# Attention and two feed-forward layers: weight sums moved between engines, attention paced denser, PSUM banks shared earlier

## The chip, the cores and the metric

The kernel runs on one core of a Trainium2 chip. The metric is the device time of one execution in microseconds. Three runs of the kernel before gave 716.2, 716.98 and 717.67 us; the median is 716.98. One more execution was taken with the profiler.

## The reference

Three stages, in float32, each feeding the next:

```python
# attention: B, H, S, D = 2, 8, 768, 64; six sign bits per row choose a bucket
mask = q_bucket[:, :, :, None] == k_bucket[:, :, None, :]
scores = np.where(mask, scale * q @ k.T, -1e9)
attn = exp(scores - max) / (sum + 1e-9)
x = (attn @ v) as 1536 tokens x 512
# layer 1: 512 -> 2048 -> 512
h = x @ w_in;  g = where(h > 0, h, exp(min(h, 0)) - 1);  x = g @ w_out
# layer 2: 512 -> 2048 -> 512
h = x @ w_in2; g = s * max(h, 0)**2 + b;                 out = g @ w_out2
```

The inputs arrive as float64 words. The kernel reads them as pairs of 32-bit integers and rebuilds float32 from them on the chip.

## The kernel before, in words

**Precision.** Every matmul of the layers works on operands split into two float16 parts, high and low. Three products (high x high, high x low, low x high) stand for one. ScalarE mostly writes the high part (a copy to float16), and VectorE or GpSimd writes the low part (the value minus the high part).

**Attention** goes in 96 units of 128 queries of one head. `u_s` (L352) computes the scores s into PSUM, `u_soft` (L362) takes them out on VectorE with the maximum (L368) and applies the exponential on ScalarE (L370), `u_split` (L374) writes ph as high part on ScalarE (L389) and low part on GpSimd (L392) and sends a transposing DMA from SP's queue, and `u_av` (L397) multiplies with v into xacc (L412). `u_norm` (L425) finishes 128 tokens. Units 48 to 95 are batch 1.

**Layer 1** (`moe1`, L627) goes in six blocks of 256 tokens, each `up(i)` and then `down(i)`, both in 16 slots of 12 matmuls on TensorE (L533). A pair of slots of `up` fills one PSUM tile h; `act1` (L536) turns it into g: e on ScalarE (L541 and, in blocks 0, 1, 4 and 5, its scaling L543), g on VectorE (L550), the high part gh on ScalarE (L553), the low part gl on GpSimd (L556). A `down` fills two PSUM tiles x2p in 8 slots each, and ScalarE writes each to x (L676). The PSUM tiles h and x2p come from a ring of pools (`Ring`, L117, kind "m"); it has three banks from the time that layer 1's weights are decoded.

**Weaving.** After each slot, `model_kernel` (L1049 on) adds the slot's cost to a credit, and runs half units of attention for half of `sc` each. `sc` is 1.2 for the first 16 slots, then `STEP_COST` 2.5:

```python
cost = 12 * (n / 2400 + .003)
credit += cost
sc = STEP_COST if ks >= SC_N else SC0
while live["att"] and credit >= sc / 2 and may_step():
    credit -= sc / 2
    att_step()
```

The order on each engine is made when the program is built, by a list scheduler that goes by readiness and by a priority, which is the place in the program. So the weave sets priorities, and what is ready can go ahead.

**Layer 2's weights.** Once attention is exhausted, its pools are closed, four PSUM pools `ps_y` are opened (before, only layer 2 used them), and a stream `ws2` of 32 chunks begins (`w_stream`, L170). A step of it loads one chunk (a DMA of SP, three buffers), decodes the chunk loaded two steps earlier with three VectorE instructions (L194, L195, L197; a "triple" below), and takes the one decoded in the step before. A step is taken in two of seven slots until `F0` = 18 steps are made. All of a step's instructions have their priority put back by `D2` = 200 places.

`wo_chunks` (L711) and `wi_chunks` (L738) say what taking means. Layer 2 is computed with seven block products in place of eight, so its weights are needed as blocks and as four sums of blocks. Two chunks make a pair. ScalarE scales each chunk (L716, L743). Then four 128x256 sums go into a tile tt, which has one buffer (L725 to L728 for w_out2, L751 to L754 for w_in2), all on GpSimd. Then high and low parts are written in three pieces of 256, 512 and 1024 columns for w_out2 (L733 and L734; the first two low parts on VectorE, the last, from tt, on GpSimd) and of 512, 256 and 1024 for w_in2 (L758 and L759, all low parts on GpSimd). Eight pairs of w_out2 and eight of w_in2 are made. The converted w_in2 tile has two buffers.

**Layer 2's x operands.** `x_piece` (L591) makes the sums of x blocks (L607) and low parts (L604) on VectorE and the high parts on ScalarE (L601). They are written over layer 1's weights `wi`, so each waits until up(5) has read what it overwrites. The last of them wait for the end of layer 1.

**Layer 2.** `up2` (L765) runs eight blocks j of 14 products (L809), six banks in use; the first product of each side also presets a bank (L814). After each product it takes steps of the weight stream up to a goal between `fed_at[j]` and `fed_at[j+1]`. `finish` (L782) and `product` (L801) empty the banks on ScalarE (L788, L816, L819) and VectorE (L796, L821, L825). The banks are the list `ps_m + ps_y` in this order: a of both sides, c of both, b of both. `down2` (L870) then makes the output (L948).

Of the kernel before, what the change touches and what calls it, by code (L numbers as in the profile page):

```python
# [12 lines left out]
ALU = mybir.AluOpType  # L13
# [33 lines left out]
GUEST = [(0, "k"), (0, "q"), (2, "k"), (2, "q"), (0, "v"), (1, "v")]  # L47
NS = 2
NX = 1
F0 = 18  # L50
Y2 = 4
D2 = 200
DA = 4
# [4 lines left out]
WEV = lambda k: k % 3  # L58
W2EV = lambda k: k % 7 in (0, 3)
STEP_COST = 2.5  # L60
SC0 = 1.2
SC_N = 16
PRE = 4
# [4 lines left out]
def model_kernel(tc, q, k, v, proj, w_in, w_out, w_in2, w_out2, s2, b2, sel, pop, eye, out):  # L68
    nc = tc.nc
# [23 lines left out]
    with ExitStack() as base:  # L93
# [21 lines left out]
        ps_m = []  # L115
# [25 lines left out]
        ring = Ring()  # L141
# [329 lines left out]
        nxt = {"s": 0, "av": 0, "soft": [], "split": [], "lag": LAG0}  # L471
# [239 lines left out]
        def wo_chunks(dram, wq, lp):  # L711
            w = dram.bitcast(I32)
            kept = {}

            def take(f, a):
                nc.scalar.activation(out=a, in_=a, func=ACTF.Copy, scale=SW)  # L716
                kept[f] = a
                if f < KF // 2:
                    return
                f -= KF // 2  # L720
                a, c = kept.pop(f), kept.pop(f + KF // 2)
                b11, b12, b21, b22 = a[:, :256], a[:, 256:], c[:, :256], c[:, 256:]
                t = lp.tile([128, 4, 256], F32, tag="tt", name="tt")
                t1, n2, t3, n4 = (t[:, x, :] for x in range(4))
                nc.gpsimd.tensor_tensor(out=t1, in0=b12, in1=b11, op=ALU.subtract)  # L725
                nc.gpsimd.tensor_tensor(out=n2, in0=t1, in1=b22, op=ALU.subtract)
                nc.gpsimd.tensor_tensor(out=t3, in0=b22, in1=b12, op=ALU.subtract)
                nc.gpsimd.tensor_tensor(out=n4, in0=b21, in1=n2, op=ALU.add)  # L728
                hi, lo = wq
                c = c.rearrange("p (x n) -> p x n", x=2)  # L730
                for eng, o, src in ((nc.vector, slice(0, 1), a[:, None, :256]), (nc.vector, slice(1, 3), c),
                                    (nc.gpsimd, slice(3, 7), t)):
                    nc.scalar.activation(out=hi[:, o, f, :], in_=src, func=ACTF.Copy)  # L733
                    eng.tensor_tensor(out=lo[:, o, f, :], in0=src, in1=hi[:, o, f, :], op=ALU.subtract)  # L734
            order = [f for x in range(KF // 2) for f in (x, x + KF // 2)]
            return [(lambda a, f=f: take(f, a), w[128 * f:128 * f + 128, :]) for f in order]

        def wi_chunks(dram, wt, lp, wjp):  # L738
            w = dram.bitcast(I32)
            kept = {}  # L740

            def take(f, a):
                nc.scalar.activation(out=a, in_=a, func=ACTF.Copy, scale=SW)  # L743
                kept[f] = a
                if f % 2 == 0:
                    return
                a, c = kept.pop(f - 1), kept.pop(f)
                a11, a12, a21, a22 = a[:, :256], a[:, 256:], c[:, :256], c[:, 256:]
                t = wjp.tile([128, 4, 256], F32, tag="tt", name="tt")
                s1, m2, s3, s4 = (t[:, x, :] for x in range(4))  # L750
                nc.gpsimd.tensor_tensor(out=s1, in0=a21, in1=a22, op=ALU.add)  # L751
                nc.gpsimd.tensor_tensor(out=m2, in0=a11, in1=s1, op=ALU.subtract)
                nc.gpsimd.tensor_tensor(out=s3, in0=a11, in1=a21, op=ALU.subtract)
                nc.gpsimd.tensor_tensor(out=s4, in0=a12, in1=m2, op=ALU.add)  # L754
                o = wt[f // 2] = lp.tile([128, 2, 7, 256], F16, tag="wi2", name="wi2", bufs=2)
                a = a.rearrange("p (x n) -> p x n", x=2)
                for x, src in ((slice(0, 2), a), (slice(2, 3), a22[:, None, :]), (slice(3, 7), t)):
                    nc.scalar.activation(out=o[:, 0, x, :], in_=src, func=ACTF.Copy)  # L758
                    nc.gpsimd.tensor_tensor(out=o[:, 1, x, :], in0=src, in1=o[:, 0, x, :], op=ALU.subtract)  # L759
            return [(lambda a, f=f: take(f, a), w[:, 256 * f:256 * f + 256].rearrange("(k p) n -> p k n", p=128))  # L760
                    for f in range(KF)]
# [3 lines left out]
        def up2(wt, home, g, g3, banks, stream, fed, fed_all, ahead):  # L765
# [67 lines left out]
            def quads(j):  # L833
                Qs = [dict(j=j, p=p, banks={}, pools={}) for p in range(2)]
                for x in "acb":
                    for Q in Qs:
                        Q["pools"][x] = free.pop(0)
                        Q["banks"][x] = Q["pools"][x].tile([128, 512], F32, tag="m", name=x + "2")[:, :NT]
                return Qs
# [2 lines left out]
            std = [(x, n) for n in (1, 5, 6, 2, 7, 3, 4) for x in range(2)]  # L842
            begin = [(0, 1), (1, 1), (0, 5), (1, 5), (0, 6), (0, 2), (1, 2), (1, 6), (0, 7), (0, 3), (1, 7), (0, 4), (1, 3), (1, 4)]
            end = [(0, 1), (0, 5), (1, 1), (0, 6), (0, 2), (1, 5), (0, 7), (1, 6), (0, 3), (0, 4), (1, 7), (1, 2), (1, 3), (1, 4)]
            fed_at = [F0, 22, 24, 28, 30, 32, 34, 36, 36]
            step, over = 0, False
            for j in range(N8):
                Qs = quads(j)
                for e, (x, n) in enumerate(begin if j == 0 else end if j == N8 - 1 else std):
                    product(Qs[x], n)  # L850
                    for o in range(4):
                        run(o)
                    tick()
                    goal = fed_at[j] + (fed_at[j + 1] - fed_at[j]) * (e + 1) // 14
                    if j == 6:
                        goal = min(36, 34 + e)
                    while not over and fed[0] < goal:
                        if next(stream, 0) == 0:
                            over = True
                            fed_all()  # L860
                        fed[0] += 1
                    if j == N8 - 1 and e == 9:
                        ahead(3)
# [126 lines left out]
        if True:  # L990
# [59 lines left out]
            for ks, cost in enumerate(moe1(wi, wo, gp, next_gp, tmp, tmpg, att_step, home)):  # L1050
                if WEV(ks):
                    w1_step()
                credit += cost
                sc = STEP_COST if ks >= SC_N else SC0
                while live["att"] and credit >= sc / 2 and may_step():
                    credit -= sc / 2
                    att_step()
                if not live["att"] and ws2 is None:
                    exst.close()
                    ast.close()  # L1060
                    ps_y = [pool(pst, f"ps_y{i}", 1, space=PSUM) for i in range(Y2)]
                    wqp = right(wqst, "wq", 1)
                    wq = [wqp.tile([128, 7, KF // 2, DM // 2], F16, name=f"wq{x}") for x in "hl"]
                    lp = right(late, "late", 1)
# [9 lines left out]
                    sb["s"], sb["b"], sb["2b"] = (sbs[:, x:x + 1] for x in range(3))  # L1074
                    co = wo_chunks(w_out2, wq, wjp)
                    ci = wi_chunks(w_in2, wi2, lp, wjp)
                    ch = co[:10] + ci[:4] + co[10:14] + ci[4:8] + co[14:] + ci[8:]
                    ws2 = w_stream(ch, wraw,
                                   lambda: (wjp.tile([128, 512], F32, tag="wa", name="wa", bufs=3),
                                            ps_x.tile([128, 512], F32, tag="x", name="wx")), delay=D2)  # L1080
                elif ws2 is not None and W2EV(ks) and fed2[0] < F0:
                    next(ws2)
# [81 lines left out]
```

## Time and profile before

| | |
|---|---|
| median of three runs | 716.98 us (716.2 to 717.67) |
| profiled execution, its own time | 716.12 us |
| its span, first to last instruction | 714.3 us |
| mean granted TensorE clock | 0.983 |
| busy: TensorE matmuls | 647.5 us (91%) |
| busy: VectorE, ScalarE, GpSimd | 528.0, 474.0, 376.2 us (74%, 66%, 53%) |

The span is what the engines' instructions cover; 1.8 us of the execution's time lie around it. Busy times overlap between engines. A matmul's end is modelled and reaches into the next one, so a TensorE that is busy all the time is not one at its peak, but one that waits for nothing. The granted clock is a share of full speed: 1.00 is 2.4 GHz, and a mean below it says that for a part of the stretch the clock stood at 1.2 GHz. In the rows, "a <- b" is the tile written and the tiles read; at the end of a row, "<-" names what ended the idle time before it.

### The profile page before, as it was taken

To read this page: it belongs to the slowest core of one execution; us is meant where nothing else is said; L and a number is where in the kernel's file an instruction comes from. 1 tells how busy PE (TensorE), PEld (TensorE's weight loads), DVE (VectorE), ACT (ScalarE), POOL (GpSimd) and SP (SyncE) were. 2 spreads that over 40 slices of the span, in tenths; PEclk is the share of its full clock that TensorE was granted. 3 is DMA by queue.
4 is the path that set the end of the run, shared out by engine and by line. 5 is a ranking of instruction groups with operands and counts; after the bars stand their busy time and mean duration, and the time that the engine had idled before them with its cause. 6 is when DMAs were issued, how large, how long until landed. Compare 5 with 4: busy or idle time off the path is not lost.

```text
span 714.3 us, 15720 instructions
## 1 busy us (share of the span) xinstructions
PE 647.5 (91%) x6290; PEld 514.0 (72%) x6290; DVE 528.0 (74%) x876; ACT 474.0 (66%) x810; POOL 376.2 (53%) x323
## 2 busy tenths in 40 slices
PE   2789779888889899999999998877999999999998
PEld 0368657767667688888888886664566667888887
DVE  5688899888888568645742599999777667999820
ACT  2897679863798888656756667756677677556410
POOL 1257778873445479756854488886577741000000
PEclk9999979999999999999999999999999999999999
DMA  9974699999899698676759554223234002301011
GB/s 233 264 218 137 164 210 248 206 204 254 153 205 215 105 166 162 130 123 112 127 111 124 144 175 144 60 67 110 88 119 150 23 34 82 129 30 46 30 42 34
DMA packets 209625, 96.05 MB, mean 134 GB/s; under 512 B 172176, under 2 KB 205712, under 8 KB 209552
## 3 DMA queue, kind: packets, MB, share of 16 engines
q1 hardware_dynamic: 208960, 94.92, 59.3%
q8 instruction: 49, 0.80, 0.4%
q14 instruction: 24, 0.20, 0.1%
q10 hardware_dynamic: 592, 0.14, 0.1%
HBM read 46.27 MB, written 6.29 MB: 74 GB/s over the span
## 4 chain that ended last, share of the span: by engine, by line
PE 46%; DVE 8%; ACT 6%; issue 3%; POOL 2%; DMA 1%; SPq 0%; DVEq 0%; ACTq 0%; POOLq 0%
PE y L948 15%; PE a L809 8%; PE x2p L533 6%; PE h L533 5%; PE c L809 4%; PE s L358 3%; PE xacc L412 3%; PE b L809 2%; DVE x L607 1%; DVE e L548 1%; DVE wil L604 1%; ACT p L370 1%; ACT ph L389 1%; DVE wx L195 1%; DVE wa L197 1%
## 5 line engine op out<-in xcount | busy, mean ns | idle before, releaser
L392 POOL TENSOR_TENSOR ph<-p,ph 128x768 f16<-128x768 f32 x80 | 132.8, 1665 | 69.0 <-ACT ph L389 50.3
L533 PE MATMUL h<-x,wih 128*128 128x256 f16 x768 | 133.8, 278 | 4.7 <-DVE g L550 4.6
L368 DVE TENSOR_SCALAR_CACHE_REDUCE p<-s 128x768 f32<-128x768 f32 x96 | 91.2, 952 | 57.9 <-PE s L358 54.0
L370 ACT ACTIVATE p<-p,mx 128x768 f32<-128x768 f32 x96 | 89.2, 929 | 49.9 <-DVE mx L369 43.5
L533 PE MATMUL x2p<-gh,woh 128*128 128x256 f16 x384 | 103.8, 273 | 3.7 <-DVE g L550 2.7
L533 PE MATMUL h<-x,wil 128*128 128x256 f16 x384 | 106.6, 278 | 0.0
L533 PE MATMUL x2p<-gl,woh 128*128 128x256 f16 x384 | 104.3, 273 | 1.7 <-POOL gl L556 1.7
L533 PE MATMUL x2p<-gh,wol 128*128 128x256 f16 x384 | 104.4, 273 | 1.2 <-DVE wol L204 1.2
L809 PEld LDWEIGHTS <-wi 128*128 128x128 f16 x672 | 66.3, 99 | 49.0 <-issue 7.0
L533 PEld LDWEIGHTS <-wih 128*128 128x128 f16 x768 | 75.5, 100 | 20.4 <-DVE g L550 6.7
L533 PEld LDWEIGHTS <-woh 128*128 128x128 f16 x768 | 74.6, 98 | 16.4 <-issue 3.9
L358 PE MATMUL s<-k,q 128*128 128x512 f16 (+1 forms) x384 | 80.8, 336 | 4.6 <-DVE p L368 4.3
L412 PE MATMUL xacc<-vv,pt 128*128 128x64 f16 x1440 | 57.9, 195 | 18.9 <-DMA pt<-ph 18.8
L556 POOL TENSOR_TENSOR gl<-g,gh 128x512 f16<-128x512 f32 x48 | 59.2, 1233 | 28.5 <-ACT gh L553 27.9
L412 PEld LDWEIGHTS <-pt 128*128 128x128 f16 x1440 | 53.7, 99 | 26.5 <-DMA pt<-ph 23.3
L389 ACT ACTIVATE ph<-p 128x768 f16<-128x768 f32 x80 | 66.4, 836 | 5.7 <-DMA pt<-ph 4.8
L358 PEld LDWEIGHTS <-q 128*128 128x128 f16 x384 | 34.4, 100 | 23.1 <-issue 9.2
L194 DVE TENSOR_SCALAR wx<-wraw 128x512 int32<-128x512 int32 x64 | 44.5, 695 | 5.7 <-DMA wraw<-in_moe_w_out 5.0
L197 DVE SCALAR_TENSOR_TENSOR wa<-wraw,wx 128x512 int32<-128x512 int32 x64 | 43.7, 682 | 5.1 <-POOL wi L759 2.3
L809 PE MATMUL a<-wih,wi 128*128 128x384 f16 x160 | 46.3, 329 | 1.2 <-ACT x L676 1.2
L195 DVE SCALAR_TENSOR_TENSOR wx<-wraw,wx 128x512 int32<-128x512 int32 x64 | 44.2, 691 | 0.9
L533 PEld LDWEIGHTS <-wol 128*128 128x128 f16 x384 | 37.6, 98 | 8.0 <-issue 2.0
(186 smaller groups left out, 1536.0 us busy)
## 6 DMA issues: line engine op xcount, KB each, us to landing
wraw<-in_moe_w_in SPq DMA_DIRECT2D x32, 512.0 KB, 3.8
wraw<-in_moe_w_out SPq DMA_DIRECT2D x32, 512.0 KB, 4.2
g<-x SPq DMA_DIRECT2D x16, 192.0 KB, 1.9
x<-g SPq DMA_DIRECT2D x4, 768.0 KB, 5.2
out<-y SPq DMA_DIRECT2D x10, 256.0 KB, 2.0
raw<-in_k SPq DMA_DIRECT2D x6, 384.0 KB, 4.5
raw<-in_q SPq DMA_DIRECT2D x6, 384.0 KB, 4.9
v<-in_v SPq DMA_DIRECT2D x4, 384.0 KB, 4.7
```

The source lines that it names most:

```text
L195: nc.vector.scalar_tensor_tensor(out=x, in0=low, scalar=29, in1=x, op0=ALU.logical_shift_right, op1=ALU.bitwise_or)
L197: nc.vector.scalar_tensor_tensor(out=a, in0=top, scalar=-0x40000000, in1=x, op0=ALU.bitwise_and, op1=ALU.bitwise_or)
L358: nc.tensor.matmul(p[:, a0:a1], w[b, hp][:, j, c, :], kf[:, a0:a1], start=(x == 0), stop=(x == 1))
L368: nc.vector.tensor_scalar(f, sps.pop(u), CLAMP, None, op0=ALU.min, op1=ALU.min, accum_out=mx)
L370: nc.scalar.activation(out=f, in_=f, func=ACTF.Exp, scale=-sm / (SQ * SQ), bias=mx, accum_out=sums[b, c][:, h:h + 1])
L389: nc.scalar.activation(out=t[:, 0, :], in_=f, func=ACTF.Copy)
L392: nc.gpsimd.tensor_tensor(out=t[:, 1, :], in0=f, in1=t[:, 0, :], op=ALU.subtract)
L412: nc.tensor.matmul(acc, o[:, C * x + cc, :], vv[:, j, cc, y, :], start=(z == 0 and cc == 0), stop=(z == 2 and cc == C - 1))
L533: nc.tensor.matmul(p, ws[a](kk), xs[b](kk), start=(kk == 0 and z == 0), stop=(kk == n_kk - 1 and z == 2))
L556: nc.gpsimd.tensor_tensor(out=gl, in0=t["g"], in1=gh, op=ALU.subtract)
L809: nc.tensor.matmul(d, w[:, wz, WI[n], kk * 128:kk * 128 + 128], home[p, xn, xz][:, kk, :], start=first and k == 0, stop=k == 3 * K1 - 1, s ...
L948: nc.tensor.matmul(p, a[:, xa, kk, :], wq[y][:, WQ[n], kk, :], start=first and k == 0, stop=k == 3 * K2 - 1, skip_group_check=True)
```

## The change

- The four sums of each w_out2 pair go from GpSimd to VectorE; the first two low parts of the pair go from VectorE to GpSimd.
- The four sums of the first two w_in2 pairs (f = 1 and 3) go from GpSimd to VectorE.
- From unit 60 on a unit of attention costs 2.0 credits in place of 2.5.
- When attention is exhausted, the ring of layer 1's PSUM tiles gets `ps_m + ps_y`, seven banks in place of three, and its count starts anew.
- Layer 2's chunks come in another order after the first 14: two of w_out2 and two of w_in2 in turn, in place of four and four.
- 17 steps of the stream in place of 18 ahead of `up2`; within `up2` the goal after block 0 is 20 in place of 22, and goals are reached earlier within a block (rounded up instead of down, nearly).

```diff
-F0 = 18
+F0 = 17
...
+SC2, U2 = 2.0, 60
...
-                nc.gpsimd.tensor_tensor(out=t1, in0=b12, in1=b11, op=ALU.subtract)
-                nc.gpsimd.tensor_tensor(out=n2, in0=t1, in1=b22, op=ALU.subtract)
-                nc.gpsimd.tensor_tensor(out=t3, in0=b22, in1=b12, op=ALU.subtract)
-                nc.gpsimd.tensor_tensor(out=n4, in0=b21, in1=n2, op=ALU.add)
+                nc.vector.tensor_tensor(out=t1, in0=b12, in1=b11, op=ALU.subtract)
+                nc.vector.tensor_tensor(out=n2, in0=t1, in1=b22, op=ALU.subtract)
+                nc.vector.tensor_tensor(out=t3, in0=b22, in1=b12, op=ALU.subtract)
+                nc.vector.tensor_tensor(out=n4, in0=b21, in1=n2, op=ALU.add)
...
-                for eng, o, src in ((nc.vector, slice(0, 1), a[:, None, :256]), (nc.vector, slice(1, 3), c),
+                for eng, o, src in ((nc.gpsimd, slice(0, 1), a[:, None, :256]), (nc.gpsimd, slice(1, 3), c),
                                     (nc.gpsimd, slice(3, 7), t)):
...
-                nc.gpsimd.tensor_tensor(out=s1, in0=a21, in1=a22, op=ALU.add)
-                nc.gpsimd.tensor_tensor(out=m2, in0=a11, in1=s1, op=ALU.subtract)
-                nc.gpsimd.tensor_tensor(out=s3, in0=a11, in1=a21, op=ALU.subtract)
-                nc.gpsimd.tensor_tensor(out=s4, in0=a12, in1=m2, op=ALU.add)
+                eng = nc.vector if f < 4 else nc.gpsimd
+                eng.tensor_tensor(out=s1, in0=a21, in1=a22, op=ALU.add)
+                eng.tensor_tensor(out=m2, in0=a11, in1=s1, op=ALU.subtract)
+                eng.tensor_tensor(out=s3, in0=a11, in1=a21, op=ALU.subtract)
+                eng.tensor_tensor(out=s4, in0=a12, in1=m2, op=ALU.add)
...
-            fed_at = [F0, 22, 24, 28, 30, 32, 34, 36, 36]
+            fed_at = [F0, 20, 24, 28, 30, 32, 34, 36, 36]
...
-                    goal = fed_at[j] + (fed_at[j + 1] - fed_at[j]) * (e + 1) // 14
+                    goal = fed_at[j] + ((fed_at[j + 1] - fed_at[j]) * (e + 1) + 11) // 14
...
-                sc = STEP_COST if ks >= SC_N else SC0
+                sc = SC0 if ks < SC_N else STEP_COST if nxt["s"] < U2 else SC2
...
+                    ring.use(m=ps_m + ps_y)
...
-                    ch = co[:10] + ci[:4] + co[10:14] + ci[4:8] + co[14:] + ci[8:]
+                    ch = co[:10] + ci[:4] + co[10:12] + ci[4:6] + co[12:14] + ci[6:8] + co[14:16] + ci[8:10] + ci[10:12] + ci[12:14] + ci[14:16]
```

## Rows read from the trace of the kernel before

**Rows 1.** Windows: stretch, length, busy us (instructions) per engine, clock, DMA share, GB/s.
```profile
255.00:300.00 45.00, 43.51 (x563) 36.30 (x561) 33.86 (x68) 35.16 (x63) 38.27 (x26) 1.00 0.90 159
...
400.00:429.50 29.50, 29.50 (x271) 26.31 (x269) 25.82 (x43) 19.70 (x34) 21.41 (x20) 1.00 0.62 193
429.50:486.00 56.50, 46.01 (x394) 38.94 (x392) 54.62 (x66) 37.15 (x62) 48.40 (x39) 0.97 0.29 88
486.00:500.00 14.00, 9.82 (x48) 5.06 (x46) 13.90 (x23) 8.91 (x19) 8.28 (x9) 0.88 0.37 112
500.00:520.00 20.00, 20.00 (x125) 11.96 (x123) 14.02 (x26) 12.38 (x28) 9.72 (x10) 1.00 0.31 99
520.00:560.00 40.00, 40.00 (x248) 24.09 (x247) 30.93 (x55) 28.85 (x58) 30.95 (x32) 1.00 0.35 109
```

The engines of a window stand in the order PE, PEld, DVE, ACT, POOL.

**Rows 2.** Waits of PE, 425 to 500 us: total us, times, longest.
```profile
PE h L533 <- DVE g L550: 4.6, 3, 2.9
PE x2p L533 <- DVE g L550: 2.7, 1, 2.7
PE b L809 <- DVE wih L604: 2.0, 1, 2.0
PE b L814 <- ACT wih L601: 1.9, 1, 1.9
PE a L809 <- ACT x L676: 1.2, 1, 1.2
PE x2p L533 <- POOL gl L556: 0.9, 1, 0.9
PE c L809 <- DVE wih L604: 0.6, 1, 0.6
```

**Rows 3.** Lines by form on DVE, 429.5 to 500 us: busy us, mean ns | idle before.
```profile
L607 DVE TENSOR_TENSOR x<-x 128x512 f32<-128x512 f32 x8 | 9.7, 1211 | 0.0
...
L194 DVE TENSOR_SCALAR wx<-wraw 128x512 int32<-128x512 int32 x12 | 8.2, 686 | 0.1
...
L607 DVE TENSOR_TENSOR x<-x 128x256 f32<-128x256 f32 x8 | 7.0, 869 | 0.0
...
L734 DVE TENSOR_TENSOR wql<-wa,wqh 128x512 f16<-128x512 f32 x4 | 4.1, 1030 | 0.1
...
L734 DVE TENSOR_TENSOR wql<-wa,wqh 128x256 f16<-128x256 f32 x3 | 1.2, 412 | 0.0
```

**Rows 4.** Timeline of DVE: start, us, instruction [idle before].
```profile
403.15 0.69 DVE L194 TENSOR_SCALAR wx<-wraw 128x512 int32<-128x512 int32 x1 [2.98 <-DMA wraw<-in_moe_w_out]
...
420.10 0.42 DVE L734 TENSOR_TENSOR wql<-wa,wqh 128x256 f16<-128x256 f32 x1
...
428.61 0.69 DVE L197 SCALAR_TENSOR_TENSOR wa<-wraw,wx 128x512 int32<-128x512 int32 x1
...
446.84 2.28 DVE L607 TENSOR_TENSOR x<-x 128x256 f32<-128x256 f32 x1
```

**Rows 5.** Timeline of POOL at the same time as the last of these.
```profile
446.71 2.12 POOL L734 TENSOR_TENSOR wql<-tt,wqh 128x1024 f16<-128x1024 f32 x1
```

**Rows 6.** Chain that ended last: layer 1's matmuls between two units, start and us.
```profile
300.33 2.62 PE x2p L533 x24
304.12 2.62 PE x2p L533 x24
```

**Rows 7.** Timeline of PE: attention's last product, and the start of block 5.
```profile
394.52 0.57 PE L412 MATMUL xacc<-vv,pt 128*128 128x64 f16 x14
...
429.50 0.38 PE L533 MATMUL h<-x,wih 128*128 128x256 f16 x2
```

**Rows 8.** Lines by form on POOL, 429.5 to 500 us.
```profile
L556 POOL TENSOR_TENSOR gl<-g,gh 128x512 f16<-128x512 f32 x8 | 10.4, 1295 | 4.2 <-ACT gh L553 4.2
...
L725 POOL TENSOR_TENSOR tt<-wa 128x256 f32<-128x256 f32 x4 | 4.6, 1155 | 0.2
...
L759 POOL TENSOR_TENSOR wi<-wa,wi 128x512 f16<-128x512 f32 x2 | 2.5, 1239 | 0.0
```

## The prediction

> **What bounds the kernel now.** The page's slices come first: TensorE is nearly full from the slice at 300 us to the end, except in four slices near 430 to 500 us. The windows view [rows 1] turns that into numbers: TensorE is busy 29.50 of 29.50 us at 400 to 429.5, then 46.01 of 56.5, then 9.82 of 14, then 20.00 of 20. The busy engine of the gap is VectorE: 54.62 of 56.5 and 13.90 of 14 us. In the same stretch GpSimd is busy 48.40 and 8.28 us. TensorE's waits at 425 to 500 us [rows 2] say on what: 4.6 us before h and 2.7 before x2p for g on VectorE, 2.0 + 0.6 for wih on VectorE, 1.9 for wih on ScalarE, 1.2 for x from the last PSUM tile, 0.9 for gl, and two of 0.4 that are not shown. Sum 14.7 us. The same view lists no wait of TensorE between 300 and 425 us or from 500 us on, so every microsecond won before 500 us arrives at the end, and nothing else in the second half can be won.
>
> What fills VectorE there is in its lines by form [rows 3]: the x sums and low parts (L607 alone: 9.7 and 7.0 us), twelve decode triples of layer 2's weights (L194 is 8.2 us in 12, and L195 and L197 match it, so 2.07 us a triple), and low parts of weight sums (L734). Many of these are stretched: a 128x256 f32 operation took 0.42 us at 420.10 and 2.28 us at 446.84 [rows 4], where GpSimd ran one of 2.12 us from 446.71 [rows 5]. So there are three loads: the x work, which has to be there; layer 2's weights, which need not; and the collisions with GpSimd.
>
> **The change part by part.**
>
> *Denser attention.* From unit 60 a unit costs 2.0 credits in place of 2.5, and a slot of 12 matmuls brings 12*(256/2400+0.003) = 1.316. 36 units then free 18 credits, or 13.7 slots; counting the loop slot by slot, attention is exhausted at slot 122 in place of 137, 15 slots earlier. A slot is 1.31 us of TensorE (24 matmuls take 2.62 [rows 6]), so attention's last product moves from 394.5 [rows 7] to some 375 us, and the first decode of layer 2's weights from 403.15 [rows 4] to some 383.5. TensorE's total work is the same; block 5 still starts near 429.5 us [rows 7]. The price is the unit's period: 3.79 us now (300.33 to 304.12 [rows 6]), 3.15 after. Each unit also sends a transposing DMA from SP. The nearest row at such a density is 255 to 300 us [rows 1]: TensorE 43.51 of 45, DMA share 0.90. Lower bound 0 (no stall at 3.79); upper bound 1.49/45 over the roughly 110 us that become dense, 3.6. I take 1, since that stretch also carried batch 1's preparation.
>
> *Weights earlier.* Before, 9 triples were decoded by 429.5 us (403.15 to 428.61 are the first and last of them [rows 4]), in 26.3 us, 2.93 us each; 12 more ran between 429.5 and 500. After, 46 us lie ahead of 429.5. At the same pace that is 15.7 triples; the pairs of w_out2 become dearer (below), 3.0 to 3.9 us a triple, 15.3 down to 11.7. I take 14. The first block of layer 2 feeds the stream to 20 steps in place of 22, that is 18 triples decoded, so some 4 remain in the gap in place of 12. Eight triples are 8 x 2.07 = 16.6 us of VectorE taken out of it. The loads (one per step on SP's queue) move with them; attention is over by then, so they pass no transpose, and DMA share was 0.62 at 400 to 429.5 [rows 1].
>
> *Sums on VectorE, low parts on GpSimd.* Per pair of w_out2 GpSimd loses four sums (L725 1.155 us in this stretch [rows 8], the three like it near 1) and gains a 128x512 and a 128x256 low part, the wide one like L759's 1.239 [rows 8], the narrow one at some 0.8 as half its columns: about -4.2 + 2.0 = -2.2 us. VectorE loses 1.03 + 0.41 [rows 3] and gains four 128x256 sums: 0.42 each if alone [rows 4], 0.87 as L607's stretched mean [rows 3], so +0.2 to +2.0 us, of which I take 0.8: GpSimd is less loaded than in L607's stretch. For the two pairs of w_in2 with f below 4 there is no low part to give away: +1.7 to +3.5 us each, while GpSimd loses some 3.9. Most of it falls ahead of 429.5, where TensorE waits for nothing. Left in the gap are about two pairs, at most 7 us, against the 5.3 us of L734 [rows 3] that leave VectorE. GpSimd's work in the gap is gl (10.4 us [rows 8]) and otherwise weights; with 4 triples in place of 12 these fall by more than half, so the stretched x operations should shorten: L607's eight narrow ones at the 0.42 of 420.10 [rows 4] would be 3.4 in place of 7.0 us, the eight wide ones at twice that 6.7 in place of 9.7; I take some 4 of these 6.6 us and nothing for L604. So VectorE loses 16.6 + 5.3 + 4 - 7 = 19 us in the gap, more than the 14.7 us that TensorE waits: it stops being the bound, and the waits can go but for the chains named next. A sum needs the one tile of sums (a single buffer), so it waits until GpSimd has finished the previous low part; before, GpSimd itself stood there, now VectorE would, with g behind it. The order of the queues decides that; it is one of the rivals.
>
> A rule of the Trainium skill speaks against this part. SBUF — State Buffer, section "Who interferes with whom", calls the port pair that VectorE and GpSimd share an exclusive lock, taken for a whole instruction by a VectorE operation with two SBUF inputs or by a GpSimd one, the other blocking fully. The trace agrees: the 2.28 us at 446.84 [rows 4] end within 0.3 us of GpSimd's 2.12 [rows 5]. By the rule a sum costs anything from 0.42 to 2.3 us, by what GpSimd started before it, and the two pairs left in the gap could cost 18 us in place of 7.
>
> *Seven banks.* Block 5's h tiles no longer wait for g of the third tile before: the 4.6 us before h, and the 1.9 us of a preset of b queued in front of them, lose their cause. TensorE runs ahead, and the backlog shows at the end of up(5) instead: the last g passes e, its scaling, g, gh and gl before x2p's last quarter needs it. Three quarters of the first product (3 x 1.31 = 3.9 us) cover about that chain; with one x operation of 2 us in front on VectorE, 2 us remain. Counting takes, layer 1's last tile is the 21st, which falls on the bank of layer 2's first product; it must be emptied first, as in the 1.2 us of [rows 2], though products of other banks can go before. And the first products that filled gaps before can no longer do so. For this and the last x operands I leave 2 us at the start of layer 2 (lower bound 0; upper bound the 4.2 us of wih, x and x2p there [rows 2]).
>
> *Order of chunks, F0 and the feeding.* The weights of each block of layer 2 come at or ahead of their place before, and the total is unchanged. Layer 2's up stage gets about 3 to 4 more triples and one or two pairs more: 8 to 12 us on VectorE, which idles 6.0 us at 500 to 520 and 9 at 520 to 560 [rows 1]. Covered, so 0; if the cover fails, see the second rival.
>
> **Clock.** The granted clock was 0.97 and 0.88 in the two windows with gaps and 1.00 around them [rows 1]: TensorE was at 1.2 GHz in place of 2.4 for a part of them, after it had stood idle. That is (1 - 0.97) x 56.5 + (1 - 0.88) x 14 = 3.4 us at most; as much of it lay in idle time, I take 1 us as won (bounds 0 and 3.4).
>
> **Sum.** 14.7 + 1 - 2 (end of up(5)) - 2 (start of layer 2) - 1 (dense attention) = 10.7 us. Against the profiled execution's 716.12 us (span 714.3, 1.8 around it) that is 705.4; the median of the runs is 716.98, 0.86 higher, so 706.3.
>
> **Rivals.**
> *VectorE stays the bound* (chance 0.25). The sums collide with GpSimd, or VectorE stands at the single tile of sums, and g comes late again; seven banks only move the wait from h to x2p. For it: VectorE at 97% in the gap [rows 1] and the 2.28 us row. Against: 16.6 us go. Price: 40 sums at 0.45 more (0.87 against 0.42), 18 us, a third in the gap: 6 us. Gain 10.7 - 6 = 4.7, time 712.3. (The lock rule of the Trainium skill, SBUF — State Buffer, would make this case the likelier one.)
> *Layer 2's start chokes* (0.14), the slower case. Triples and sums that left the gap meet VectorE's evictions in the first two blocks of layer 2's up stage. The price if all of it meets the first 20 us: 4 triples, 8.3 us, and 8 sums at 1.6 (midway between 0.87 and 2.28), 12.8, together 21.1, against 6.0 us of idle VectorE time [rows 1]: 15.1 us of new waits, and 716.98 - 10.7 + 15.1 = 721.4. It decides once the excess passes 10.7 us. Against: no TensorE wait there now, and GpSimd's loss of sums.
> *The stall only moves* (0.11). The seven banks let layer 1 take those on which layer 2's first products ran early; the 14.7 us return as waits for x operands, whose last parts depend on layer 1's end. Then 716 to 717.5. That the schedule ignores the denser setting is excluded by the loop count.
>
> **How the numbers follow.** My forecast has 0.50. Its own bounds: all waits and the whole clock term won, 14.7 + 3.4 = 18 (699); the least, 14.7 with 3.6 lost to the density, 4.2 at layer 2's start and 4 at up(5)'s end, no clock term, 2.9 (714). The range reaches to 716 for the first rival and part of the third, and down to 701. About 0.2% (1.4 us) is what a measurement can tell here. Faster: 0.50 + 0.25 = 0.75; within: 0.11; slower: 0.14.
>
> **What would show it.** The windows view: TensorE's idle time from block 5's start to layer 2's full pace falls from 14.7 to about 4 us, VectorE below 95% there. The waits: no h behind g; what is left is x2p behind g or gl, and a or b behind x operands. Unit period near 3.15 us after unit 60, attention's end near 375 us, the first decode near 383, TensorE still full in between. L734's low parts appear on GpSimd near 1.2 and 0.8 us, the sums on VectorE at 0.4 to 0.9. Wrong would be: waits for pt behind its DMA above 3 us after unit 60, VectorE sums above 1 us on average, x2p behind g above 5 us, or new waits in layer 2.

## The result, and the profile after

Fourteen runs of the kernel after have a median of 719.75 us (717.32 to 722.34), against 716.8 us of fourteen runs of the kernel before on the same chip: ratio 1.0051, 95% interval 1.0033 to 1.007. The change costs 0.5%; the forecast was a gain of 10.7 us. The profiled execution took 721.49 us (span 719.7, mean clock 0.979). It lies 1.7 us above its median, and the profiled one before, 716.12 us, 0.7 us below its own; so the two traces differ by 5.4 us where the medians differ by 2.95, and what follows accounts for the traces.

The page's busy times of the kernel after:

```profile
PE 647.8 (90%) x6290; PEld 513.5 (71%) x6290; DVE 535.8 (74%) x900; ACT 471.2 (65%) x810; POOL 355.8 (49%) x299
```

TensorE does what it did; GpSimd lost 20 us and VectorE gained 8. The windows of the kernel after, cut where its stages begin: 392 is up(4), 413 down(4), 440 up(5), 461 down(5), 494 layer 2 (engines in the order PE, PEld, DVE, ACT, POOL, then clock, DMA share, GB/s):

```profile
300.00:392.00 92.00, 89.28 (x1104) 76.25 (x1102) 46.37 (x99) 50.34 (x86) 52.92 (x37) 0.98 0.81 134
392.00:413.00 21.00, 21.00 (x195) 18.84 (x193) 20.64 (x35) 16.27 (x30) 13.21 (x11) 1.00 0.50 151
413.00:440.00 27.00, 21.74 (x193) 18.58 (x192) 26.48 (x38) 16.12 (x28) 19.26 (x16) 1.00 0.43 133
440.00:461.00 21.00, 21.00 (x195) 18.84 (x193) 20.71 (x34) 14.22 (x24) 11.32 (x8) 1.00 0.42 132
461.00:494.00 33.00, 25.51 (x200) 20.57 (x198) 26.43 (x31) 17.89 (x31) 16.80 (x12) 0.84 0.06 17
494.00:510.00 16.00, 16.00 (x102) 9.74 (x100) 7.41 (x16) 8.38 (x19) 1.99 (x2) 1.00 0.04 13
510.00:544.00 34.00, 31.05 (x189) 18.12 (x187) 29.24 (x53) 24.35 (x50) 19.85 (x19) 1.00 0.42 124
```

The one gap of [rows 1] has become two, one in down(4) and one in down(5), with a smaller one in layer 2. Both `up` stages run in 21.00 us without a pause. VectorE is full from 392 to 461; before, it was full only from 429.5 on [rows 1]. TensorE's waits, 255 to 717 us, of the kernel after (total us, times, longest):

```profile
PE x2p L534 <- POOL gl L557: 9.0, 7, 2.8
PE xacc L413 <- DMA pt<-ph: 4.9, 6, 2.5
PE x2p L534 <- ACT gh L554: 3.7, 3, 1.6
PE a L811 <- ACT b L818: 2.1, 2, 1.3
PE a L811 <- POOL wi L761: 0.7, 1, 0.7
```

Every wait of [rows 2] before h is gone, as forecast, and so are those for wih and x, of which the forecast left 2 us. In their place x2p waits 12.7 us for g's parts (5.3 of it at 400 to 430 us, where the kernel before lists no wait, 7.5 at 430 to 500), attention 4.9 us for its transposing DMA, and layer 2's up stage 2.8 us.

Block 5 now starts at 440.1 us, in place of 429.50 [rows 7]:

```profile
440.11 0.38 PE L534 MATMUL h<-x,wih 128*128 128x256 f16 x2
```

Of these 10.6 us, 5.3 are waits of down(4), 4.3 are waits for pt (4.9 in place of 0.6), and up to 1.8 are the clock (0.98 over 92 us); the three are each an upper share, since they add up to 11.4. From there to the end of the span the kernel after takes 279.6 us and the kernel before 284.8: 5.2 us shorter, near 14.7 - 7.5 - 2.8 = 4.4. So a gain of 5 us at the end of layer 1 is paid with 10.6 ahead of it, where the forecast had nothing but 1.

Next, why g is late. The sums on VectorE, 380 to 500 us, kernel after (ns, least/median/most):

```profile
L726 DVE TENSOR_TENSOR tt<-wa x6: 778/1090/1384, 393.7 to 453.4; 128x256 f32<-128x256 f32 x6
L727 DVE TENSOR_TENSOR tt<-tt,wa x6: 409/410/420, 396.4 to 456.8; 128x256 f32<-128x256 f32 x6
L728 DVE TENSOR_TENSOR tt<-wa x6: 412/1374/1378, 396.8 to 454.7; 128x256 f32<-128x256 f32 x6
L729 DVE TENSOR_TENSOR tt<-wa,tt x6: 410/568/1328, 398.7 to 459.3; 128x256 f32<-128x256 f32 x6
```

The same operation takes 0.41 us or 1.37. The four medians add up to 3.4 us a pair; so do the means, since the 24 sums take 20.3 us together. VectorE is nowhere idle ahead of a sum, so it does not stand at the one tile tt, as that rival of the prediction had it. Two of the sums in VectorE's timeline of the kernel after:

```profile
431.54 1.19 DVE L726 TENSOR_TENSOR tt<-wa 128x256 f32<-128x256 f32 x1
432.66 1.37 DVE L728 TENSOR_TENSOR tt<-wa 128x256 f32<-128x256 f32 x1
```

and GpSimd's at the same time:

```profile
431.30 1.16 POOL L735 TENSOR_TENSOR wql<-wa,wqh 128x512 f16<-128x512 f32 x1
432.41 1.34 POOL L761 TENSOR_TENSOR wi<-wa,wi 128x512 f16<-128x512 f32 x1
```

Each sum starts 0.25 us after a low part has started on GpSimd and ends 0.3 us after it ends: it has stood still for most of that low part. Other stretched sums stand in the same way beside gl, which GpSimd computes from two tiles in SBUF. What this does to ScalarE's queue, from its timeline in up(5) of the kernel after:

```profile
442.02 0.63 ACT L744 ACTIVATE wa<-wa 128x512 f32<-128x512 f32 x1 [2.77 <-DVE wa L198]
...
448.50 0.63 ACT L717 ACTIVATE wa<-wa 128x512 f32<-128x512 f32 x1 [2.53 <-DVE wa L198]
...
450.51 0.58 ACT L542 ACTIVATE e<-h 128x512 f32<-128x512 f32 x1
```

The first h tile of up(5) is complete near 440.1 + 2.6 = 442.7 us, and the first e starts at 450.51. In these 7.8 us ScalarE is idle for 3.0 (0.51 and 2.53): it stands in its queue, at scalings of weight chunks that VectorE has not decoded yet, with e behind them. The rest it works, nearly all of it at weights. The order was put down when the program was built; that it reckoned with sums that don't stretch is inferred. With seven banks TensorE doesn't notice during up(5); it runs ahead to down(5) and waits there.

A late g is not all of it. In down(4), 4.8 of the 5.3 us end with a gh or gl that was computed as soon as its g or gh was there. Of the 7.5 us of down(5), 6.2 (1.97, 2.82 and 1.38) end with a gl whose gh had been ready for 1.3 to 2.4 us, while GpSimd worked at layer 2's weights. The longest:

```profile
463.48 0.62 ACT L554 ACTIVATE gh<-g 128x512 f16<-128x512 f32 x1
...
464.52 1.18 POOL L753 TENSOR_TENSOR tt<-wa 128x256 f32<-128x256 f32 x1
465.66 0.91 POOL L755 TENSOR_TENSOR tt<-wa 128x256 f32<-128x256 f32 x1
466.54 1.66 POOL L557 TENSOR_TENSOR gl<-g,gh 128x512 f16<-128x512 f32 x1
...
468.25 0.37 PE L534 MATMUL x2p<-gl,woh 128*128 128x256 f16 x1 [2.82 <-POOL gl L557]
```

### The profile page after: what moved, and what is told of

The parts are those of the page before. It is cut to its first block, busy times and chain, and to the rows that moved or that the text cites. A ratio compares the mean times of both kernels' runs of the same rounds, so it can differ in the third digit from the quotient of the medians.

```text
span 719.7 us, 15721 instructions
## 1 busy us (share of the span) xinstructions
PE 647.8 (90%) x6290; PEld 513.5 (71%) x6290; DVE 535.8 (74%) x900; ACT 471.2 (65%) x810; POOL 355.8 (49%) x299
## 4 chain that ended last, share of the span: by engine, by line
PE 49%; DMA 14%; DVE 13%; issue 9%; ACT 9%; POOL 5%; SPq 1%; DVEq 0%; POOLq 0%; ACTq 0%
PE y L950 15%; PE x2p L534 8%; PE a L811 6%; DMA pt<-ph 6%; PE h L534 5%; PE s L359 4%; PE c L811 3%; DMA wraw<-in_moe_w_out 3%; PE xacc L413 2%; ACT p L371 2%; POOL ph L393 2%; DVE wx L195 2%; DVE wa L198 2%; DVE wx L196 2%; DMA q<-src 2%
## 5 line engine op out<-in xcount | busy, mean ns | idle before, releaser
L534 PE MATMUL x2p<-gl,woh 128*128 128x256 f16 x384 | 106.4, 278 | 9.0 <-POOL gl L557 9.0
L534 PE MATMUL x2p<-gh,woh 128*128 128x256 f16 x384 | 106.2, 279 | 4.4 <-ACT gh L554 3.7
L534 PE MATMUL x2p<-gh,wol 128*128 128x256 f16 x384 | 106.5, 278 | 0.9 <-DVE wol L205 0.9
```

What stands on the lines that cost most here:

```text
L534: nc.tensor.matmul(p, ws[a](kk), xs[b](kk), start=(kk == 0 and z == 0), stop=(kk == n_kk - 1 and z == 2))
```

## The experiments

Ratios are against the kernel before, run on the same chip, with 95% intervals. The theory: collisions of VectorE's two-input operations with GpSimd's make VectorE late, the in-order queues carry this on to g, and the banks only move the place of the wait. The rivals: one single part is to blame (the denser pace, the banks, the order of the chunks), or GpSimd's mere load is.

**One part left out of the kernel after.** Four kernels, on one chip. `l_dense`:

```diff
-SC2, U2 = 2.0, 60
+SC2, U2 = 2.5, 60
```

> The changed kernel with attention's old pace (2.5 credits a unit throughout); the rest of the change stays. Theory W (the early end of attention puts layer 2's weight stream into up(4), whose g then comes late): TensorE's waits of 5.3 us for gh and gl at down(4) go, as do the 4.9 us for pt behind its DMA of theory D (the denser units outrun their transposing DMA). W and D together: 719.7 becomes 709 to 714. Theory N (seven banks only move the wait from h to x2p): the wait at down(4) stays, 717 to 720.

`l_banks` leaves out the line `ring.use(m=ps_m + ps_y)`.

> The changed kernel without the seven banks: layer 1's tiles stay in three. N: the 5.3 and 7.5 us of x2p at down(4) and down(5) turn back into less than that of h behind g, 713 to 717. W: the g's are as late as before, so h waits in up(4) and up(5) in place of x2p and the first products of layer 2 fill some gaps again: 718 to 722.

`l_sums` gives the sums back to GpSimd, and two low parts to VectorE:

```diff
-                nc.vector.tensor_tensor(out=t1, in0=b12, in1=b11, op=ALU.subtract)
...
+                nc.gpsimd.tensor_tensor(out=t1, in0=b12, in1=b11, op=ALU.subtract)
...
-                for eng, o, src in ((nc.gpsimd, slice(0, 1), a[:, None, :256]), (nc.gpsimd, slice(1, 3), c),
+                for eng, o, src in ((nc.vector, slice(0, 1), a[:, None, :256]), (nc.vector, slice(1, 3), c),
...
-                eng = nc.vector if f < 4 else nc.gpsimd
+                eng = nc.gpsimd
```

> The changed kernel with the sums back on GpSimd and the two low parts back on VectorE. If the sums on VectorE are what makes g late (they collide with GpSimd, 0.42 to 1.4 us each between 393 and 432 us): x2p's waits at down(4) fall by half or more, 713 to 716. If it is the weight stream as such (W): the waits stay within 2 us, 718 to 722.

`l_order` restores the order of the chunks, `F0 = 18`, `fed_at` and the goal.

> The changed kernel with the old order of chunks, 18 steps ahead of layer 2, and the old feeding. If these cause the 2.8 us of waits in layer 2 (a behind b's copy on ScalarE and behind a weight's low part on GpSimd): about 716 to 717. If they do nothing: 718 to 721. W, D and N all say that the waits before 500 us stay.

| left out | median us | ratio |
|---|---|---|
| denser pace | 721.74 | 1.0094 (1.0071 to 1.0118) |
| seven banks | 720.21 | 1.0070 (1.0049 to 1.0092) |
| sums on VectorE | 717.41 | 1.0038 (1.0016 to 1.0060) |
| order, feeding | 722.94 | 1.0104 (1.0085 to 1.0124) |

No part, left out, brings the kernel back below the one before. The four ran side by side: without the sums on VectorE the kernel is 2.8 to 5.5 us faster than without any other part, but still at 1.0038, between the two times expected. Whether a kernel of the table is faster or slower than the kernel after (1.0051, measured apart from these, against other runs of the kernel before) is not shown; `hold`, below, says how far such ratios scatter. In `l_sums` x2p still waits 10.7 us. VectorE's low parts are the stretched operations there (L735 of 128x256 takes 0.90 us on average at 380 to 460 us, against 0.42 in [rows 4]), and VectorE also stands idle for GpSimd's sums, because they hold the buffers that its decodes write; its waits, 385 to 500 us of `l_sums`:

```profile
DVE wa L198 <- POOL tt L728: 5.6, 2, 3.2
...
DVE wa L198 <- POOL tt L755: 3.5, 1, 3.5
```

Without the banks, h waits for g again (3.7 us), and b 3.8 us for wih: the wait has gone back to where it was.

**One part alone, on the kernel before.** `o_banks`, `o_dense`, `o_sums` and `o_order` make one of the four edits each (the lines of the diff ahead of the prediction).

> The kernel before with the seven banks alone. As the prediction had it (the banks remove h's waits for g and 2 us come back): 710 to 713 against 714.8 to 717. Theory N (the wait only moves from h in up(5) to x2p in down(5)): within 2 us of the kernel before, with 8 us or more of x2p waits.

> The kernel before with the denser attention alone. As the prediction had it (density costs 1 us, weights come earlier and leave room in VectorE's full stretch): 706 to 712. Theory D (the transposing DMAs are outrun, 3 to 5 us and a lowered clock) with the weights' stream now in up(4) (W): 716 to 722, h behind g in up(4).

> The kernel before with the sums on VectorE and the low parts on GpSimd alone. As predicted (GpSimd's relief outweighs): 713 to 716. Theory L (eight sums' worth of collisions more, 1.7 us a pair of w_out2): 717 to 721.

> The kernel before with the new order of chunks, 17 steps and the new feeding alone. Leaving them out of the changed kernel cost 3 to 4 us, so 711 to 715 if that gain stands alone; as predicted (nothing): within 1.5 us of the kernel before.

| alone | median us | ratio |
|---|---|---|
| seven banks | 717.96 | 1.0038 (1.0017 to 1.0059) |
| denser pace | 720.1 | 1.0053 (1.0030 to 1.0076) |
| sums on VectorE | 721.01 | 1.0069 (1.0044 to 1.0094) |
| order, feeding | 714.42 | 0.9993 (0.9969 to 1.0017) |

Three of the parts cost 0.4 to 0.7% each, and the order by itself is worth nothing, as forecast; what it is worth inside the change is open. They do not add up (1.5% against the 0.5% of the whole). Parts that share a bottleneck would behave so, but this doesn't show that they share one. TensorE's waits in `o_dense`, 255 to 717 us:

```profile
PE h L534 <- DVE g L551: 9.2, 3, 4.9
PE x2p L534 <- DVE g L551: 5.4, 2, 3.0
```

Here the weights come earlier with the sums still on GpSimd, and g is later than before (4.6 and 2.7 in [rows 2]); VectorE waits for GpSimd's sums as in `l_sums`, 9.1 us. In `o_banks` h waits for nothing and x2p 7.0 us for gl. One part by itself turns one wait into another.

**Holding the weights back.** `hold` lets the stream of layer 2's weights start no earlier than slot 137, where it started before the change:

```diff
-                elif ws2 is not None and W2EV(ks) and fed2[0] < F0:
+                elif ws2 is not None and ks >= 137 and W2EV(ks) and fed2[0] < F0:
```

> The changed kernel, but no step of layer 2's weights before slot 137, where they began before; attention still ends at slot 122. Theory W (weights in up(4) make g late there): the 5.3 us of x2p at down(4) fall below 1.5, 712 to 717. If they are due to the seven banks or to attention's density alone, they stay, 718 to 722.

It gave 721.76 us, 1.0087 (1.0059 to 1.0116), and tells nothing of its question: the order of the instructions on VectorE and on SP came out the same as in the kernel after, because the scheduler places what is ready ahead of what the loop names first. So it is in effect the kernel after measured a second time, against other runs of the kernel before, and 1.0087 against 1.0051 is how far such ratios scatter.

**Taking the collisions away.** `nolow` writes the low parts of layer 2's weights as zeros, which reads nothing from SBUF:

```diff
-                    eng.tensor_tensor(out=lo[:, o, f, :], in0=src, in1=hi[:, o, f, :], op=ALU.subtract)
+                    nc.gpsimd.memset(lo[:, o, f, :], 0.0)
...
-                    nc.gpsimd.tensor_tensor(out=o[:, 1, x, :], in0=src, in1=o[:, 0, x, :], op=ALU.subtract)
+                    nc.gpsimd.memset(o[:, 1, x, :], 0.0)
```

> The changed kernel with every low part of layer 2's weights set to zero by GpSimd (it reads nothing), in place of computed; the low parts of w_in2 and w_out2 are left out of the result. Theory L (VectorE, full from 390 to 452 us, falls behind its planned place because its two-input operations wait for GpSimd's; ScalarE's weight scalings wait for it and hold up the e's queued behind them, the first e of up(5) by 8 us): VectorE's sums drop to 0.42 us, the first e of up(5) starts within 4 us of its h tile, x2p's waits at down(4) and down(5) fall from 12.8 below 6: 707 to 714. If it is the amount of work on VectorE and not the collision: 716 to 720.

705.84 us, 0.9862 (0.9825 to 0.9900), near the forecast's 706.3 (0.985 of the kernel before). But the memsets are also shorter than the low parts (0.95 us for 128x1024 in place of 2.14), so GpSimd's load could be the cause as well as the collisions. `busy` makes each memset twice:

> As the run with zeroed low parts, but each zeroing done twice, so that GpSimd is occupied about as long as by the computed low part (2 x 0.95 us against 2.14), still without reading. The low parts of layer 2's weights are left out. Theory L (GpSimd's reads stretch VectorE's two-input operations): the time stays near the first one, 704 to 710, and VectorE's sums stay at 0.42 us. Theory O (what counted was GpSimd's occupation, with gl queued behind the low parts): most of the gain goes, 714 to 719.

708.01 us, 0.9894 (0.9856 to 0.9932). Windows 390 to 452 us of the kernel after:

```profile
390.00:452.00 62.00, 56.74 (x513) 49.97 (x511) 60.66 (x92) 39.30 (x69) 38.66 (x30) 1.00 0.47 144
```

and of `busy`:

```profile
390.00:452.00 62.00, 59.25 (x539) 52.52 (x537) 60.96 (x103) 48.86 (x86) 41.23 (x63) 1.00 0.51 154
```

GpSimd is busier in `busy` than in the kernel after, 41.23 us against 38.66, VectorE is as full, and yet VectorE gets 103 instructions done in place of 92. Its sums there, 390 to 452 us of `busy`:

```profile
L727 DVE TENSOR_TENSOR tt<-tt,wa x6: 411/417/643, 391.4 to 442.3; 128x256 f32<-128x256 f32 x6
L728 DVE TENSOR_TENSOR tt<-wa x6: 409/419/1396, 391.7 to 442.6; 128x256 f32<-128x256 f32 x6
L729 DVE TENSOR_TENSOR tt<-wa,tt x6: 407/418/781, 392.6 to 443.5; 128x256 f32<-128x256 f32 x6
L726 DVE TENSOR_TENSOR tt<-wa x5: 418/426/1183, 395.5 to 441.3; 128x256 f32<-128x256 f32 x5
```

The medians are back at 0.42 us; only a few are long. So it isn't that GpSimd is busy, it is what GpSimd reads. That rules out the load as the main cause. One rival stays: with memsets the scheduler made another plan (VectorE's order in `nolow` and in `busy` leaves that of the kernel after at the thirteenth instruction, counted from the first sum), so a part of the gain can be the plan's. In `nolow` the first e of up(5) follows its first h by 4.0 us (430.49 to 434.49) in place of 10.4:

```profile
434.49 0.58 ACT L542 ACTIVATE e<-h 128x512 f32<-128x512 f32 x1
```

**The sums fed from PSUM.** In `ps4` ScalarE writes most of the scaled chunks to the four PSUM banks of `ps_y` that seven banks would have taken, for the first five pairs of w_out2 and the first two of w_in2, so that each sum has at most one operand in SBUF. The low parts of these chunks go to VectorE. Cut to w_out2:

```diff
-                nc.scalar.activation(out=a, in_=a, func=ACTF.Copy, scale=SW)
-                kept[f] = a
+                early = f % (KF // 2) < 5
+                if early:
+                    z = wps()
+                    if f >= KF // 2:
+                        nc.scalar.activation(out=z, in_=a, func=ACTF.Copy, scale=SW)
+                        kept[f] = z, z
+                    else:
+                        nc.scalar.activation(out=z[:, slice(0, 256)], in_=a[:, slice(0, 256)], func=ACTF.Copy, scale=SW)
+                        nc.scalar.activation(out=a[:, slice(256, 512)], in_=a[:, slice(256, 512)], func=ACTF.Copy, scale=SW)
+                        kept[f] = (z, a)
...
-                for eng, o, src in ((nc.gpsimd, slice(0, 1), a[:, None, :256]), (nc.gpsimd, slice(1, 3), c),
+                near = nc.vector if early else nc.gpsimd
+                for eng, o, src in ((near, slice(0, 1), a[:, None, :256]), (near, slice(1, 3), c),
...
-                    ring.use(m=ps_m + ps_y)
```

> The changed kernel without seven banks; for the first five pairs of w_out2 and the first two of w_in2 ScalarE writes three of the four scaled blocks to the idle PSUM banks, so that each sum and each block's low part on VectorE reads SBUF once and PSUM once; those low parts are on VectorE. Only the low part of the sums is left to GpSimd. By theory L these operations cannot be held up by GpSimd: sums at 0.42 to 0.5 us, h behind g in up(4) below 2 us, 708 to 714 in spite of 1.1 us more of VectorE's work a pair. If VectorE's amount of work is the bound: 718 to 724.

709.45 us, 0.9917 (0.9884 to 0.9950). The sums on VectorE in `ps4`, 380 to 500 us:

```profile
L738 DVE TENSOR_TENSOR tt<-wa,wps x5: 410/415/422, 389.7 to 420.7; 128x256 f32<-128x256 f32 x5
...
L740 DVE TENSOR_TENSOR tt<-wps,wa x5: 416/417/424, 391.9 to 422.0; 128x256 f32<-128x256 f32 x5
...
L740 DVE TENSOR_TENSOR tt<-wa x1: 1376/1376/1376, 446.4 to 446.4; 128x256 f32<-128x256 f32 x1
...
L741 DVE TENSOR_TENSOR tt<-wa,tt x1: 1060/1060/1060, 450.7 to 450.7; 128x256 f32<-128x256 f32 x1
```

With one operand in PSUM (wps) none of the 28 sums is longer than 0.424 us. Eight of them start while GpSimd is at a gl, which reads SBUF, and do not wait for it. One of these, and the gl beside it:

```profile
405.33 0.41 DVE L738 TENSOR_TENSOR tt<-wa,wps 128x256 f32<-128x256 f32 x1
...
405.13 1.16 POOL L557 TENSOR_TENSOR gl<-g,gh 128x512 f16<-128x512 f32 x1
```

The one later pair, with both operands in SBUF (wa), has sums of 1.376 and 1.060 again, both begun inside a gl. Against `l_banks` (1.0070), which also has three banks and the dense pace, `ps4` differs in where these operands and low parts are. Two variants on another chip: `ps4_nd` is `ps4` at the old pace of 2.5, and `ps2` gives layer 1's ring two more banks and the weights two.

> The previous PSUM version with attention's old pace. The weights then begin 15 slots later. If the early weights are worth what the prediction said once the collisions are gone (VectorE's full stretch emptied): 713 to 717, with more waits in up(5) and at layer 2's start. If the density costs as much as it brings (3 us for pt behind its DMA and a lowered clock): within 2 us of 709.5.

> The previous PSUM version with two of the four spare banks for the weights' blocks and two for layer 1's tiles (five in its ring). If more banks remove h's waits for g once VectorE keeps its plan, as the prediction had it: h behind g (1.7 in up(4), 4.0 in up(5)) goes, 705 to 709. Theory N (the wait moves to x2p): 709 to 712; with two banks the next pair of weights may also wait for the last, 711 to 714.

They gave 706.99 us, 0.9879 (0.9858 to 0.9900), and 708.2 us, 0.9895 (0.9870 to 0.9921): no order among the three could be read from this. So the two parts were crossed on one chip: `q_b3` is `ps4_nd`, `q_b3d` is `ps4`, `q_b5d` is `ps2`, and `q_b5` is `ps2` at 2.5.

> Sums fed from PSUM, three banks for layer 1, the old pace of 2.5: the corner without the change's two other timing parts, near 0.988. This is the base of a square of four kernels that differ only in the pace (2.5 or 2.0) and in the banks of layer 1's ring (three or five). If the forecast's terms hold without collisions, five banks take away the waits before h (4 us) and the denser pace moves VectorE's work ahead for about 1 us of stalls, and this corner is the slowest of the four by 3 to 5 us. If both parts only move waits, all four lie within 2 us.

> The same with the denser pace. If density is worth something once VectorE's sums run undisturbed, 1 to 3 us below q_b3. If its stalls behind the transposing DMAs (2.7 us in one profile) eat what it brings, equal to it or up to 2 us above.

> Five banks, old pace. If banks help once g comes in time, 2 to 4 us below q_b3, with no wait before h and at most 3 us before x2p. If the wait only moves, within 1 us of q_b3, with x2p waiting 3 us or more behind gl.

> Five banks and the denser pace. If both terms hold they add up: 3 to 6 us below q_b3, near 0.980. If each only moves waits, within 2 us of q_b3, near 0.989.

| | pace 2.5 | pace 2.0 |
|---|---|---|
| three banks | 708.69, 0.9913 (0.9882 to 0.9944) | 710.22, 0.9938 (0.9908 to 0.9967) |
| five banks | 711.9, 0.9963 (0.9940 to 0.9985) | 706.94, 0.9885 (0.9863 to 0.9907) |

Neither expectation holds: the parts neither add up nor do nothing. TensorE's waits from 255 to 717 us in `q_b3`:

```profile
PE h L534 <- DVE g L551: 4.6, 2, 2.3
...
PE x2p L534 <- POOL gl L557: 1.2, 2, 0.8
```

in `q_b5`:

```profile
PE x2p L534 <- ACT gh L554: 5.5, 5, 1.8
PE x2p L534 <- POOL gl L557: 3.2, 4, 0.9
```

and in `q_b5d`:

```profile
PE xacc L413 <- DMA pt<-ph: 4.8, 5, 2.6
PE x2p L534 <- POOL gl L557: 3.3, 3, 2.2
PE x2p L534 <- ACT gh L554: 1.3, 2, 1.1
```

At the old pace five banks turn 4.6 us before h into 8.7 before x2p: weights and x work still fill VectorE there (53.05 and 54.00 of 54 us at 440 to 494), and running ahead gains nothing. At the dense pace (`q_b5d`) VectorE is at 46.04 of 54 us in that window, g follows, h waits for nothing, and 4.6 us of x2p are left, with 4.8 for pt as the price of the pace. `q_b5d` lies below `q_b5`, and just below `q_b3d`, with intervals that don't overlap; the other neighbours' do. The same kernels gave 0.9879, 0.9917 and 0.9895 on other chips where `q_b3`, `q_b3d` and `q_b5d` gave 0.9913, 0.9938 and 0.9885, so the order of these three is not settled. All four lie below the kernel before, `q_b5d` lowest by its median (0.9885).

## Why the prediction was wrong, step by step

- **"Most of it falls ahead of 429.5, where TensorE waits for nothing".** This is the step that failed: work that the change puts ahead of block 5 was costed at nothing. That cover was VectorE's idle time: it was busy for 25.82 us of 29.50 just ahead of block 5 [rows 1], and the rest of the room came from the earlier end of attention. Sums and earlier triples fill it (20.64 of 21.00, 26.48 of 27.00), so g of block 4 is late too, and 5.3 us of waits appear in down(4) where the sum had none. `o_dense` shows it without a single sum on VectorE: the weights come earlier, and TensorE waits 14.6 us for g. The count itself was right: 14 triples are begun before block 5 starts, but in 50 us, not 46.
- **The sums' price.** It was set too low, within its own bounds. The prediction took 2.24 us for the four sums of a pair (1.44 + 0.8), "less loaded than in L607's stretch"; they took 3.4, 0.85 each, just inside the bound of 0.87 and short of the sign of being wrong, 1 us. Over six pairs that is 6.8 us more of VectorE's time, five of the six ahead of block 5. The Trainium skill's rule (SBUF — State Buffer, "Who interferes with whom") is that a VectorE instruction with two SBUF inputs contends with a GpSimd instruction that reads SBUF, not with one that only writes it, and that one with at most one SBUF input, outside the two-port modes, does not contend. The trace agrees in each point: 1.37 us behind a GpSimd operation that reads SBUF, 0.42 in `busy` and 0.42 in `ps4`. The prediction quoted the rule against itself and gave it a rival with 0.25. That rival, "VectorE stays the bound", names what happened; its 712.3 us too priced only the third of the sums that lie in the gap.
- **Seven banks, 2 us at the end of up(5).** Measured 7.5. The waits before h did lose their cause; the estimate reckoned with one late g, while the first e alone started 7.8 us after its tile was complete, and gl then stood behind weights on GpSimd. That banks would only move the wait to x2p stood in the first rival, at 6 us.
- **Density, 1 us.** The period was right: 342 matmuls of xacc, 18 a unit, in 300 to 360 us of the kernel after make 19 units, 3.16 us each, 3.15 forecast:

```profile
L413 PE MATMUL xacc<-vv,pt 128*128 128x64 f16 x342 | 13.2, 193 | 0.0
```

  But pt waited 4.9 us, above the stated upper bound of 3.6, and the last product of attention came at 381.1 in place of 375, the first decode at 390.12 in place of 383.5:

```profile
390.12 0.70 DVE L195 TENSOR_SCALAR wx<-wraw 128x512 int32<-128x512 int32 x1 [7.55 <-DMA wraw<-in_moe_w_out]
```

- **Clock, 1 us won.** Not won: it is 0.84 over the 33 us of down(5) and 0.98 over 92 us, after idle time of TensorE each time. At 466 to 476 us it is 0.50 and 0.54 (the lower level nearly throughout) while TensorE is busy for 6.37 of 10 us; by these figures an estimate of some 3 us lost there, besides up to 1.8 ahead of block 5, against at most 3.4 in the kernel before.
- **Start of layer 2, 2 us; order and feeding, 0.** No wait between 494 and 510 us, better than forecast, but 2.8 us between 510 and 544, where the sum had none; in size the two come out even. `o_order` is at 0.9993. The 721.4 us of the second rival are near the result, but not for its reason: layer 2 adds only 2.8 us.
- **The gain itself.** Kernels with few collisions come near the forecast of 0.985: `nolow` at 0.9862, `q_b5d` at 0.9885. That speaks for the mechanism that the prediction had beside them; that the figures meet so closely is in part luck, since both are other kernels, with other work and another order of it.

What stays open: why the pace without the banks, or the banks without the pace, costs as much as it does alone; the scheduler makes another order for each, and only the sum of their waits was read. Nor is it shown how much of the gain of `nolow`, `busy` and `ps4` is the shorter sums and how much the new order, or what the waits of down(5) would be if gl went ahead of the weights on GpSimd.

## What to carry to other kernels

Price an operation that moves to VectorE with both operands in SBUF by what GpSimd reads at that time, not by its own row: it can stand still for nearly a whole GpSimd operation (1.37 us in place of 0.41), and what queues behind it is late with it. One operand in PSUM took it out of the conflict here (0.42 us). An engine's idle time beside a full TensorE is cover only once: add up all that the change puts there before costing any of it at nothing.

## What was not expected

- One operand in PSUM made sums immune: at most 0.424 us in `ps4`, also where they start inside a gl of GpSimd; with both in SBUF 1.376 beside gl in the same kernel.
- GpSimd's memsets do not hold up VectorE's sums: a median of 0.42 us with 41.23 of 62 us of GpSimd busy.
- More free PSUM banks by themselves made the kernel before slower (1.0038), and `q_b3` too by its median (0.9913 to 0.9963, intervals that just touch): TensorE then runs further ahead of g and waits at x2p instead.
